# Differences of x by VectorE from two plain loads, EPS later, and the low parts of w_v ahead of the weight sums

## The chip, the cores and the metric

The kernel runs on one core of one Trainium2 chip. Its engines work side by side: TensorE (PE) multiplies matrices, VectorE (DVE) and ScalarE (ACT) work on elements, GpSimd (POOL) here issues the DMAs that add to what lies at their target, and SyncE (SP) issues the plain ones. Each engine takes its instructions strictly in order, so one that waits holds up all behind it. The metric is the device time of one execution in microseconds (us); lower is better.

## What is computed

One layer mixes a linear-attention block and a bilinear GLU by a gate per token. x has 2048 tokens of 512 numbers, all in fp32:

```
phi = lambda t: where(t > 0, t + 1, exp(t)) + 1e-6
q, k, v = x @ wqkv                      # 32 heads of 16
kv = einsum("bhsd,bhse->bhde", phi(k), v);   z = phi(k) summed over s
a = (phi(q) @ kv) / (phi(q) @ z + 1e-6) @ wo
b = ((x @ w_gate) * (x @ w_up)) @ w_down
g = sigmoid((x * gate_w).sum(-1))
out = g * a + (1 - g) * b
```

## The kernel before

Every fp32 operand is split into a high part that ACT writes and a low part that DVE gets by subtraction; `mm3` (L74) makes a product of three matmuls: high by high, high by low, low by high. Names that end in h or l are such parts (xc4h, wvl, fl). The large products are made by a 2x2 scheme with seven products instead of eight. Its operands of x are numbered 1 to 7 and taken in the order `UNIT = (2, 3, 4, 1, 5, 6, 7)`. Operands 2 and 5 are a block of x as it is; 1, 6 and 7 are sums of two blocks; 3 and 4 are differences (`SUMS`, L167).

The change touches **stage 1** alone (about the first 96 us): k and v of all 16 tiles of 128 tokens, phi of k, and the sums kv and z.
- First four "lead" tiles (8 to 11) go by plain products: pk with w_k, then pv with w_v.
- Then three pairs of couples go by the seven products. `couple` (L429) makes two tiles of tokens. Its step s multiplies one operand into a bank (cY, cX, cY, cR, cX, cR, cS), and `crit` moves it on: m copies the first cY on ACT, DVE makes cR from cX and m, t from cR and v, and cS from t and cX. Each step takes the product of both couples, one after the other.
- The first pair (tiles 12 to 15) uses "sub" operands, cut from the second half of the tokens: in SBUF as xo, and, split, in xb (xbh, xbl) or in soh and sol. The second and third pair (tiles 0 to 7) use the whole operands of the first half, which later serve stage 2 too: 2 and 7 in xa (xah, xal), 3 and 5 in xb, and 1, 4 and 6 in xc1, xc4 and xc6.

How an operand came about before: 3 and 4 (sub and whole) were loaded to xo, negated by ACT, and the other block was added by an accumulating DMA. The whole operands 2, 1, 5, 6 and 7 were first copied to a place in DRAM (xstage, `op_load`); where a sum was wanted, an accumulating DMA added the other block there (`op_add`), and `op_turn` (L417) fetched the result to SBUF when its place was free.

phi of a tile of k takes an exp (e) and a relu (ph) on ACT, two DVE instructions (ph, and zacc which sums for z), and last `phi_end` (L310), which adds EPS on ACT. A block of kv (pkv) needs the ended phi and v of its tiles.

The scheduling is by hand. `plan(step, fn)` puts a helper at a numbered half step of stage 1, from the table `AT`: `gsload`, `gsadd`, `gssplit` for sub operands, `goload`, `goadd`, `goturn`, `gosplit` for whole ones, `gwsplit` for sums of weights, `gkv` for kv. Steps 0 to 7 lie in the lead tiles, 8 to 21 in the first pair, 22 to 35 in the second, 36 to 49 in the third. Negative steps come ahead of all. `split_late` (L270) puts the high part at its place and the low part at the end of the half step's list. Buffers come from a list of 45 that is used in rotation (`get`, `put`), so a load also waits for the last reader of its buffer. `dma` (L82) goes through SP, `dma_add` (L85) through POOL. In the profile L52 is the matmul, L58 an ACT instruction, L61 and L64 DVE instructions.

Of the kernel before, what the change touches and what calls it, by code (L numbers as in the profile page):

```python
# [14 lines left out]
P = 128  # L15
# [8 lines left out]
CH = 512  # L24
# [12 lines left out]
UNIT = (2, 3, 4, 1, 5, 6, 7)  # L37
DOWN = (2, 6, 5, 7, 1, 3, 4)
STAYS = 1
AT = {'gsload': (-1, -1, -1, -1, -1, -1, -1), 'gsadd': (1, 0, 1, -1, 1, -1, 1), 'gssplit': (1, 3, 5, 7, 11, 13, 9), 'gmake': (-1, -1, -1, -1, -1, -1, -1, 5, -1, -1), 'gwsplit': (-1, -1, 7, 9, 11, 13, 12, 14, 15, 18), 'goload': (3, 9, 13, 7, 11, 11, 9), 'goadd': (3, 14, 17, 9, 1, 13, 17), 'gosplit': (13, 19, 25, 25, 30, 26, 30), 'gwgu': (31, 33, 49, 31, 39), 'gw0': (41, 42, 44, 42, 45, 47), 'gkv': (6, 14, 22, 27), 'by': ((16383, 10920, 10922, 10922, 2730, 10990), (8191, 10922, 10922, 10920, 11946, 10922)), 'add': (2, 4), 'high': ((2, 3, 5), (2, 3, 5), (2, 3, 4)), 'low': ((4, 4, 5), (3, 5, 6), (4, 4, 5)), 'd': (7, 8, 8, 9, 9, 9, 9, 15), 'h': (7, 7, 8, 8, 9, 13, 14, 13, 14, 15, 14, 15, 16, 15, 16, 17, 16, 17, 19), 'q0': (8, 8, 10, 11, 15, 21, 23, 24, 26, 58, 11, 11), 'q1': (8, 9, 10, 13, 24, 30, 32, 34, 38, 42, 3, 6), 'wo': (70, 6, 10, 7), 'x': (3, 4, 8, 8, 12, 12), 'o': (-3, -1, 0, 5, 35, 36, 37, 39), 'xs': (36, 41, 40, 0, 1, 2, 4), 'plain': (4, 7, 8, 1, 6, 7, 12, 12, 2, 6), 'turn': (14, 2, 18, 1, 38, 4, 50, 6), 'first': (0, 4, 1, 4, 6, 6, 14, 3, 5, 17, 15, 16, 19, 21), 'goturn': (7, 1, 5, 19, 19, 17, 20), 'gxload': (25, 27, 28, 29, 31, 34, 37, 39, 41, 43, 47, 49, 51, 54, 56, 58), 'gxsum': (32, 33, 35, 37, 33, 36, 39, 41, 43, 51, 55, 56, 57, 59, 67, 69)}  # L40


@with_exitstack
def gated_mix(ctx: ExitStack, tc, xt, xp, x, wqkv, wq, wq_add, wo, wgu, wgu_add, wdn, wdn_add, wdl, gate_w, out):
# [12 lines left out]
    def act(dst, src, func=AF.Copy, **kw):  # L57
        pin(nc.scalar.activation(dst, src, func, **kw))  # L58

    def tt(dst, a, b, op):  # L60
        pin(nc.vector.tensor_tensor(dst, a, b, op=op))  # L61
# [19 lines left out]
    def dma(dst, src):  # L81
        tc.keep_in_program_order(nc.sync.dma_start(dst, src))  # L82

    def dma_add(dst, src):
        tc.keep_in_program_order(nc.gpsimd.dma_start(dst, src, accum_op=ALU.add))  # L85
# [111 lines left out]
    def f32(w):  # L197
        return w.bitcast(F32)
# [12 lines left out]
    def later(slot, fn):  # L211
        at.setdefault(slot, []).append(fn)
# [53 lines left out]
    xs, phi, val = {}, {}, {}  # L266
# [67 lines left out]
    def plan(step, *fns):  # L334
        todo.setdefault(step, []).extend(fns)
# [33 lines left out]
        fac.setdefault(i, []).append(two)  # L369

    raw_op = {}
    xstage = {i: dram.tile([P, 2, CH], F32, name=f"xstage{i}") for i in (2, 1, 5, 6, 7)}

    def op_load(i):
        if i in xstage:
            dma(xstage[i], xp[0, SUMS[i][1]])
            return
        raw_op[i] = [get("xo") for _ in range(2)]
        for b in range(2):
            x_load(f32(raw_op[i][b]), 0, i, b)  # L380

    def op_add(i):
        if i in xstage:
            for b in range(2):
                dma_add(xstage[i][:, b], xp[0, SUMS[i][0]][:, b])
            return
        for b in range(2):
            x_add(f32(raw_op[i][b]), 0, i, b)

    ops_done = set()  # L390
    sub = {}
    PART = {A1: (B1, 0), A2: (B2, 0), B1: (B1, CH // 2), B2: (B2, CH // 2)}

    def pieces_of(w):
        return w.rearrange("p (b c) -> p b c", b=2)

    def sub_of(which):
        at_, col = PART[which]
        return xp[1, at_][:, :, col:col + CH // 2]

    def sub_load(i):
        sub[i] = get("xo")
        dma(pieces_of(f32(sub[i])), sub_of(SUMS[i][1]))

    def sub_add(i):
        one, _, minus = SUMS[i]
        if minus:
            act(f32(sub[i]), f32(sub[i]), scale=-1.0)
        dma_add(pieces_of(f32(sub[i])), sub_of(one))

    def sub_split(i):
        raw, n = sub[i], UNIT.index(i)
# [16 lines left out]
    def couple(c, tag):  # L429
        own_pair = c < KT  # L430
        ta, tb = (c, c + KT) if own_pair else (c + 8, c + 10)

        def bank_for(name):
            return unit_bank(name) if tag == "u" else bank_of("pd", name, 3)

        def operand(i, b):
            if own_pair:
                assert i in ops_done
                return [v[:, b, c * P:(c + 1) * P] for v in xc[i]]
            return [pieces_of(v)[:, b, (c - KT) * P:(c - KT + 1) * P] for v in sub[i]]  # L440

        bank, t = {}, {}

        def product(s):
            i, to = UNIT[s], "YXYRXRS"[s]
            first = i in (2, 3)
            assert len(fac[i]) == 2
            if first:
                bank[to] = bank_for(f"c{to}")
            for b in range(2):  # L450
                mm3(bank[to], operand(i, b), fac[i][b], first and b == 0, b == 1, not first, late=1)
            if not own_pair and c == KT + 1 and s > 3:
                put(*sub.pop(i))

        def crit(s):
            if s == 0:
                t["m2"] = get("m2")
                act(f32(t["m2"]), bank["Y"])
            elif s == 1:
                bank["R"] = bank_for("cR")  # L460
                tt(bank["R"], bank["X"], f32(t["m2"]), ALU.subtract)
                put(t["m2"])
            elif s == 2:
                val_of(ta, bank["Y"])
            elif s == 3:
                t["t"] = get("t")
                tt(f32(t["t"]), bank["R"], f32(val[ta]), ALU.add)
            elif s == 4:
                bank["S"] = bank_for("cS")
                tt(bank["S"], f32(t["t"]), bank["X"], ALU.subtract)  # L470
                put(t["t"])
                phi_k(tb, bank["X"])
            elif s == 5:
                phi_end(tb)
                val_of(tb, bank["R"])
            else:
                phi_k(ta, bank["S"])

        return product, crit, ta

    KV = (8, 9, 10, 11), (12, 14, 13, 15), (0, 4, 1, 5), (2, 6, 3, 7)

# [26 lines left out]
        plan(2 * n + 1, lambda t=t: phi_k(t, pk0[t]))  # L509
        plan(2 * n + 3, lambda t=t: phi_end(t))  # L510
    for k in range(KT):
        plan(-1, lambda k=k: split_v(k))
    for n, i in enumerate(UNIT):
        plan(G1["sload"][n], lambda i=i: sub_load(i))
        if i not in (2, 5):
            plan(G1["sadd"][n], lambda i=i: sub_add(i))
        plan(G1["ssplit"][n], lambda i=i: sub_split(i))
        plan(G1["oload"][n], lambda i=i: op_load(i))
        if i not in (2, 5):
            plan(G1["oadd"][n], lambda i=i: op_add(i))  # L520
        if i in xstage:
            plan(G1["oturn"][n], lambda i=i: op_turn(i))
        plan(G1["osplit"][n], lambda i=i: op_split(i))
# [48 lines left out]
    for two in (KT, KT + 1), (0, 1), (2, 3):  # L572
        pair_of = [couple(c, tag) for c, tag in zip(two, ("u", "pd"))]
        for s in range(7):
            now_slot[0] = step - STEPS
            extras(2 * step)
            for h, (product, crit, ta) in enumerate(pair_of):
                product(s)
                if h:
                    pair_of[0][1](s)  # L580
                elif s:
                    pair_of[1][1](s - 1)
                elif before:
                    last_plain()
                    before = None
                if s == 0 and ended:
                    phi_end(ended.pop(0))
                if not h:
                    kv_some(step)
            extras(2 * step + 1)  # L590
            step += 1
        ended = [ta for _, _, ta in pair_of]
        if two[0] != 2:
            pair_of[1][1](6)
    tail_crit = pair_of[1][1]
# [24 lines left out]

    begin = AT["first"]
    later(0, lambda: tail_crit(6))
    later(1, lambda: phi_end(2))
    later(1, lambda: phi_end(3))
    for s in range(step, step + 14):
        later(s - step, lambda s=s: kv_some(s))
    for k in range(2):
# [661 lines left out]
```

## Time and profile before

| | us |
|---|---|
| three runs | 593.53, 593.72, 595.69 |
| median | 593.72 |
| profiled execution | 593.48 |
| its span | 591.50 |
| second pair of couples, 50.09 to 75.17 | 25.08 |
| third pair of couples, 75.17 to 95.69 | 20.52 |

The span is what the trace covers; 1.98 us of the execution's time lie around it. All times on a trace count from the span's start. In a timeline a row reads: start, duration, engine, line, operation, what is written <- what is read, shape, and in brackets the idle time ahead of it and what ended it. In the list of waits a row reads: engine and instruction, what it waited for, us in total, times, longest. In the view by windows a row reads: stretch, its length, busy time of PE, weight loads, DVE, ACT and POOL with the count of instructions, then the clock that was granted to TensorE as a share of full speed, the DMA share and GB/s.

### The profile page before, as it was taken

The numbers are of one execution on the slowest core, as the hardware profiler recorded it, in microseconds if no ns is written. First come the engines' busy times: TensorE is split into PE (matmuls) and PEld (weight loads), VectorE is DVE, ScalarE is ACT, GpSimd is POOL, SyncE is SP. The second block draws the span as 40 slices with busy tenths as digits, with TensorE's granted clock in tenths as the row PEclk, the third lists the DMA queues.
The fourth block names the chain that finished last, engine by engine and source line by source line (L and its number), as shares of the span: only waits on it lengthen the run. The fifth ranks groups of instructions, "written<-read, shape, count | busy, mean of one in ns | idle before, by whom it ended". The sixth has DMA issues, their size and how long they took to land.

```text
span 591.5 us, 8699 instructions
## 1 busy us (share of the span) xinstructions
PE 582.2 (98%) x3047; PEld 474.6 (80%) x3047; DVE 505.0 (85%) x820; ACT 418.3 (71%) x755; POOL 67.3 (11%) x85
## 2 busy tenths in 40 slices
PE   8998999999999999999999999999999999999997
PEld 6785888777888888888888888888888888888885
DVE  7796687889698989998999976969899989889882
ACT  4588577879887878787974574887777677876300
POOL 0332000201111111111001100101101010100000
PEclk9999999999999999999999999999999999999999
DMA  8999674889797889878478356766847574631011
GB/s 280 227 271 235 205 169 148 196 209 222 183 251 178 213 203 242 192 183 212 109 219 218 115 133 188 150 139 149 188 106 162 150 159 116 134 81 35 1 74 69
DMA packets 45884, 99.29 MB, mean 168 GB/s; under 512 B 4384, under 2 KB 16928, under 8 KB 45728
## 3 DMA queue, kind: packets, MB, share of 16 engines
q0 software_dynamic: 11216, 37.49, 36.2%
q1 hardware_dynamic: 34336, 60.91, 30.0%
q8 instruction: 24, 0.39, 0.3%
q10 hardware_dynamic: 288, 0.33, 0.2%
q14 instruction: 20, 0.16, 0.1%
HBM read 87.43 MB, written 16.53 MB: 176 GB/s over the span
## 4 chain that ended last, share of the span: by engine, by line
PE 88%; ACT 4%; DMA 4%; DVE 2%; issue 1%; POOL 0%; SPq 0%; ACTq 0%; POOLq 0%
PE pdn L52 28%; PE bR L52 15%; PE bX L52 14%; PE bY L52 14%; PE bS L52 7%; PE pM L52 3%; DMA xo<-in_xp 2%; PE cR L52 2%; PE cY L52 2%; DMA wraw<-in_wqkv 2%; PE cX L52 1%; ACT e L58 1%; PE cS L52 1%; PE pkv L52 1%; ACT v L58 0%
## 5 line engine op out<-in xcount | busy, mean ns | idle before, releaser
L61 DVE TENSOR_TENSOR wcl<-wr,wch 128x512 fp32r<-128x512 f32 (+1 forms) x96 | 72.7, 772 | 5.2 <-ACT wch L58 5.2
L58 ACT ACTIVATE M<-pdn 128x512 f32<-128x512 f32 x84 | 49.9, 595 | 26.8 <-PE pdn L52 25.0
L52 PE MATMUL pdn<-hl,dh 128*128 128x512 f32 x176 | 68.5, 389 | 0.0
L52 PE MATMUL pdn<-hh,dh 128*128 128x512 f32 x176 | 68.5, 389 | 0.0
L52 PE MATMUL pdn<-hh,dl 128*128 128x512 f32 x176 | 68.5, 389 | 0.0
L58 ACT ACTIVATE wch<-wr 128x512 fp32r<-128x512 f32 (+1 forms) x96 | 66.7, 700 | 1.3 <-DMA wr<-in_wq_add 1.2
L61 DVE TENSOR_TENSOR M<-M,pdn 128x512 f32<-128x512 f32 x75 | 51.0, 681 | 13.9 <-PE pdn L52 13.7
L58 ACT ACTIVATE hh<-c 128x512 fp32r<-128x512 f32 x56 | 35.2, 629 | 37.0 <-DVE c L61 36.8
L85 POOL DMA_DIRECT2D wr<-in_wgu_add x28 | 24.3, 866 | 240.1 <-ACT wr L58 126.9
L52 PE MATMUL bX<-xbh,wch 128*128 128x512 f32 x128 | 49.8, 389 | 0.0
L52 PE MATMUL bX<-xbh,wcl 128*128 128x512 f32 x128 | 49.8, 389 | 0.0
L52 PE MATMUL bX<-xbl,wch 128*128 128x512 f32 x128 | 49.8, 389 | 0.0
L58 ACT ACTIVATE pdn<-M 128x512 f32<-128x512 f32 x61 | 35.9, 589 | 11.7 <-DVE M L61 11.7
L52 PEld LDWEIGHTS pdn<-hh,dh 128*128 128x128 f32 x176 | 33.0, 188 | 7.0
L52 PEld LDWEIGHTS pdn<-hl,dh 128*128 128x128 f32 x176 | 33.0, 188 | 7.0
L61 DVE TENSOR_TENSOR hl<-c,hh 128x512 fp32r<-128x512 f32 x56 | 38.3, 684 | 0.4
L52 PEld LDWEIGHTS pdn<-hh,dl 128*128 128x128 f32 x176 | 33.0, 188 | 6.8
L58 ACT ACTIVATE wr<-wr 128x512 f32<-128x512 f32 x64 | 36.7, 627 | 0.0
L61 DVE TENSOR_TENSOR dl<-dr,dh 128x512 fp32r<-128x512 f32 (+1 forms) x40 | 29.7, 764 | 2.3 <-ACT dh L58 2.1
L58 ACT ACTIVATE c<-bX 128x512 f32<-128x512 f32 x28 | 16.8, 600 | 20.0 <-DVE bS L61 20.0
L58 ACT ACTIVATE m<-bY 128x512 f32<-128x512 f32 x32 | 18.9, 591 | 16.5 <-PE bY L52 16.5
L58 ACT ACTIVATE dh<-dr 128x512 fp32r<-128x512 f32 (+1 forms) x40 | 27.1, 685 | 4.1 <-PE pdn L52 3.4
(265 smaller groups left out, 1597.3 us busy)
## 6 DMA issues: line engine op xcount, KB each, us to landing
wr<-in_wgu_add POOLq DMA_DIRECT2D x28, 640.0 KB, 6.4
wr<-in_wgu SPq DMA_DIRECT2D x28, 384.0 KB
dr<-in_wdn_add POOLq DMA_DIRECT2D x12, 640.0 KB, 6.9
dr<-in_wdn SPq DMA_DIRECT2D x12, 384.0 KB
xraw<-in_x SPq DMA_DIRECT2D x16, 256.0 KB
terms<-zq SPq DMA_DIRECT2D x16, 256.0 KB
zt<-terms SPq DMA_DIRECT2D x16, 256.0 KB
rb<-den SPq DMA_DIRECT2D x16, 256.0 KB
```

What stands on the lines that cost most here:

```text
L52: tc.keep_in_program_order(nc.tensor.matmul(*args, **kw))
L58: pin(nc.scalar.activation(dst, src, func, **kw))
L61: pin(nc.vector.tensor_tensor(dst, a, b, op=op))
L85: tc.keep_in_program_order(nc.gpsimd.dma_start(dst, src, accum_op=ALU.add))
```

## The change

- Of the operands of stage 1, 3 and 4 are made by DVE. Both of their blocks are loaded plainly to SBUF, and `tt(..., ALU.subtract)` takes the difference in place. The second block of each is operand 5 or 2 itself (`WITH = {4: 2, 3: 5}`), so these two are no longer loaded separately: their copies to DRAM and their turns are gone. This holds for the sub operands and for the whole ones.
- `phi_end` of the tiles of a pair of couples moves from inside the pair to steps 1 and 2 of the next pair, and after the last pair to the first two slots of stage 2. The kv blocks move a step later (`gkv`).
- The splits of w_v are planned at step -3, ahead of the sums of weights at -1.
- Loads, additions, splits and turns of the operands get new steps.

```diff
 AT = {
...
-  'gwsplit': (-1, -1, 7, 9, 11, 13, 12, 14, 15, 18),
-  'goload': (3, 9, 13, 7, 11, 11, 9), 'goadd': (3, 14, 17, 9, 1, 13, 17),
-  'gosplit': (13, 19, 25, 25, 30, 26, 30), 'gkv': (6, 14, 22, 27), 'goturn': (7, 1, 5, 19, 19, 17, 20)
+  'gwsplit': (-1, -1, 7, 9, 11, 13, 12, 14, 15, 16),
+  'goload': (0, 11, 5, 7, 0, 9, 9), 'goadd': (0, 14, 8, 9, 0, 12, 14),
+  'gosplit': (11, 19, 10, 23, 25, 27, 28), 'gkv': (6, 15, 22, 28), 'goturn': (0, 0, 0, 17, 0, 17, 20)
...
-    xstage = {i: dram.tile([P, 2, CH], F32, name=f"xstage{i}") for i in (2, 1, 5, 6, 7)}
+    xstage = {i: dram.tile([P, 2, CH], F32, name=f"xstage{i}") for i in (1, 6, 7)}
+    WITH = {4: 2, 3: 5}

     def op_load(i):
...
-        raw_op[i] = [get("xo") for _ in range(2)]
+        for k in (i, WITH[i]):
+            raw_op[k] = [get("xo") for _ in range(2)]
+            for b in range(2):
+                dma(f32(raw_op[k][b]), xp[0, SUMS[i][k != i]][:, b])
+
+    def op_add(i):
         for b in range(2):
-            x_load(f32(raw_op[i][b]), 0, i, b)
...
+            if i in xstage:
                 dma_add(xstage[i][:, b], xp[0, SUMS[i][0]][:, b])
-            return
-        for b in range(2):
-            x_add(f32(raw_op[i][b]), 0, i, b)
+            else:
+                tt(f32(raw_op[i][b]), f32(raw_op[i][b]), f32(raw_op[WITH[i]][b]), ALU.subtract)
...
     def sub_load(i):
-        sub[i] = get("xo")
-        dma(pieces_of(f32(sub[i])), sub_of(SUMS[i][1]))
+        for k in (i, WITH[i]) if i in WITH else (i,):
+            sub[k] = get("xo")
+            dma(pieces_of(f32(sub[k])), sub_of(SUMS[i][0 if k == i and i in WITH else 1]))

     def sub_add(i):
-        one, _, minus = SUMS[i]
-        if minus:
-            act(f32(sub[i]), f32(sub[i]), scale=-1.0)
-        dma_add(pieces_of(f32(sub[i])), sub_of(one))
+        if i in WITH:
+            tt(f32(sub[i]), f32(sub[i]), f32(sub[WITH[i]]), ALU.subtract)
+        else:
+            dma_add(pieces_of(f32(sub[i])), sub_of(SUMS[i][0]))
...
             elif s == 5:
-                phi_end(tb)
                 val_of(tb, bank["R"])
...
-        plan(-1, lambda k=k: split_v(k))
+        plan(-3, lambda k=k: split_v(k))
...
-                if s == 0 and ended:
+                if s in (1, 2) and ended:
                     phi_end(ended.pop(0))
...
-        ended = [ta for _, _, ta in pair_of]
+        ended = [ts[k] for k in range(2) for _, _, ts in pair_of]
...
-    later(1, lambda: phi_end(2))
-    later(1, lambda: phi_end(3))
+    for k, t in enumerate(ended):
+        later(k // 2, lambda t=t: phi_end(t))
```

What this makes of the order on the engines is seen at three places. The first is on DVE, at the beginning (from about 11 us): wkl and wvl are low parts of w_k and w_v, ws and early are sums of weights, f2l the low part of the first of these; xo<-xo is a subtraction of sub operands.

```order
 L61 TENSOR_TENSOR wkl<-wraw,wkh 128x512
+L61 TENSOR_TENSOR wvl<-wraw,wvh 128x512 x4
 L61 TENSOR_TENSOR ws<-wraw 128x512 x4
 L61 TENSOR_TENSOR early<-wraw 128x512 x3
 L61 TENSOR_TENSOR ws<-wraw 128x512 x2
-L61 TENSOR_TENSOR wvl<-wraw,wvh 128x512 x4
 L61 TENSOR_TENSOR f2l<-ws,f2h 128x512 x2
```

The four wvl pass the nine sums; behind f2l, where ph and zacc of the first lead tile stood, xo<-xo, ph and zacc, and again xo<-xo stand now.

The second place is on DVE too, in the first pair of couples. fl are low parts of sums of weights, sol of sub operands; the two cR are those of the two couples.

```order
 L61 TENSOR_TENSOR fl<-ws,fh 128x512
+L61 TENSOR_TENSOR xo<-xo 128x512 x2
 L61 TENSOR_TENSOR sol<-xo,soh 128x512
 L61 TENSOR_TENSOR fl<-ws,fh 128x512
-L61 TENSOR_TENSOR cR<-cX,m_391 128x512
+L61 TENSOR_TENSOR xc4l<-xo,xc4h 128x512 x2
+L61 TENSOR_TENSOR cR<-cX,m_395 128x512
+L61 TENSOR_TENSOR xal<-xo,xah 128x512 x2
 L61 TENSOR_TENSOR sol<-xo,soh 128x512
 L61 TENSOR_TENSOR fl<-ws,fh 128x512
 L61 TENSOR_TENSOR fl<-early,fh 128x512
-L61 TENSOR_TENSOR cR<-cX,m_416 128x512
```

Ahead of the second cR there are six instructions more: two differences for operand 4, its two low parts, and the two low parts of operand 2, which stood behind it.

The third place is on ACT, at the same time. The rows are those from the first m to where the second cR's m stands.

```order
 L58 ACTIVATE soh<-xo 128x512
 L58 ACTIVATE fh<-ws 128x512
-L58 ACTIVATE m_416<-cY 128x512
+L58 ACTIVATE xc4h<-xo 128x512 x2
+L58 ACTIVATE m_421<-cY 128x512
+L58 ACTIVATE xah<-xo 128x512 x2
 L58 ACTIVATE soh<-xo 128x512
 L58 ACTIVATE fh<-ws 128x512
```

The high parts of operand 4 stand here now; before they stood in the second pair, behind both of its m.

More of the change, by code (lines that the diff above doesn't have):

```diff
@@ L39 @@
 STAYS = 1
-AT = {'gsload': (-1, -1, -1, -1, -1, -1, -1), 'gsadd': (1, 0, 1, -1, 1, -1, 1), 'gssplit': (1, 3, 5, 7, 11, 13, 9), 'gmake': (-1, -1, -1, -1, -1, -1, -1, 5, -1, -1), 'gwsplit': (-1, -1, 7, 9, 11, 13, 12, 14, 15, 18), 'goload': (3, 9, 13, 7, 11, 11, 9), 'goadd': (3, 14, 17, 9, 1, 13, 17), 'gosplit': (13, 19, 25, 25, 30, 26, 30), 'gwgu': (31, 33, 49, 31, 39), 'gw0': (41, 42, 44, 42, 45, 47), 'gkv': (6, 14, 22, 27), 'by': ((16383, 10920, 10922, 10922, 2730, 10990), (8191, 10922, 10922, 10920, 11946, 10922)), 'add': (2, 4), 'high': ((2, 3, 5), (2, 3, 5), (2, 3, 4)), 'low': ((4, 4, 5), (3, 5, 6), (4, 4, 5)), 'd': (7, 8, 8, 9, 9, 9, 9, 15), 'h': (7, 7, 8, 8, 9, 13, 14, 13, 14, 15, 14, 15, 16, 15, 16, 17, 16, 17, 19), 'q0': (8, 8, 10, 11, 15, 21, 23, 24, 26, 58, 11, 11), 'q1': (8, 9, 10, 13, 24, 30, 32, 34, 38, 42, 3, 6), 'wo': (70, 6, 10, 7), 'x': (3, 4, 8, 8, 12, 12), 'o': (-3, -1, 0, 5, 35, 36, 37, 39), 'xs': (36, 41, 40, 0, 1, 2, 4), 'plain': (4, 7, 8, 1, 6, 7, 12, 12, 2, 6), 'turn': (14, 2, 18, 1, 38, 4, 50, 6), 'first': (0, 4, 1, 4, 6, 6, 14, 3, 5, 17, 15, 16, 19, 21), 'goturn': (7, 1, 5, 19, 19, 17, 20), 'gxload': (25, 27, 28, 29, 31, 34, 37, 39, 41, 43, 47, 49, 51, 54, 56, 58), 'gxsum': (32, 33, 35, 37, 33, 36, 39, 41, 43, 51, 55, 56, 57, 59, 67, 69)}
@@ new lines @@
+AT = {'gsload': (-1, -1, -1, -1, -1, -1, -1), 'gsadd': (1, 0, 1, -1, 1, -1, 1), 'gssplit': (1, 3, 5, 7, 11, 13, 9), 'gmake': (-1, -1, -1, -1, -1, -1, -1, 5, -1, -1), 'gwsplit': (-1, -1, 7, 9, 11, 13, 12, 14, 15, 16), 'goload': (0, 11, 5, 7, 0, 9, 9), 'goadd': (0, 14, 8, 9, 0, 12, 14), 'gosplit': (11, 19, 10, 23, 25, 27, 28), 'gwgu': (31, 33, 49, 31, 39), 'gw0': (41, 42, 44, 42, 45, 47), 'gkv': (6, 15, 22, 28), 'by': ((16383, 10920, 10922, 10922, 2730, 10990), (8191, 10922, 10922, 10920, 11946, 10922)), 'add': (2, 4), 'high': ((2, 3, 5), (2, 3, 5), (2, 3, 4)), 'low': ((4, 4, 5), (3, 5, 6), (4, 4, 5)), 'd': (7, 8, 8, 9, 9, 9, 9, 15), 'h': (7, 7, 8, 8, 9, 13, 14, 13, 14, 15, 14, 15, 16, 15, 16, 17, 16, 17, 19), 'q0': (8, 8, 10, 11, 15, 21, 23, 24, 26, 58, 11, 11), 'q1': (8, 9, 10, 13, 24, 30, 32, 34, 38, 42, 3, 6), 'wo': (70, 6, 10, 7), 'x': (3, 4, 8, 8, 12, 12), 'o': (-3, -1, 0, 5, 35, 36, 37, 39), 'xs': (36, 41, 40, 0, 1, 2, 4), 'plain': (4, 7, 8, 1, 6, 7, 12, 12, 2, 6), 'turn': (14, 2, 18, 1, 38, 4, 50, 6), 'first': (0, 4, 1, 4, 6, 6, 14, 3, 5, 17, 15, 16, 19, 21), 'goturn': (0, 0, 0, 17, 0, 17, 20), 'gxload': (25, 27, 28, 29, 31, 34, 37, 39, 41, 43, 47, 49, 51, 54, 56, 58), 'gxsum': (32, 33, 35, 37, 33, 36, 39, 41, 43, 51, 55, 56, 57, 59, 67, 69)}
@@ L377, in op_load @@
             return
-        raw_op[i] = [get("xo") for _ in range(2)]
+        for k in (i, WITH[i]):
[3 more added lines that the diff above has]
+    def op_add(i):
         for b in range(2):
-            x_load(f32(raw_op[i][b]), 0, i, b)
-    def op_add(i):
-        if i in xstage:
-            for b in range(2):
+            if i in xstage:
                 dma_add(xstage[i][:, b], xp[0, SUMS[i][0]][:, b])
-            return
-        for b in range(2):
-            x_add(f32(raw_op[i][b]), 0, i, b)
+            else:
+                tt(f32(raw_op[i][b]), f32(raw_op[i][b]), f32(raw_op[WITH[i]][b]), ALU.subtract)
     ops_done = set()
@@ L477, in crit @@
                 phi_k(ta, bank["S"])
-        return product, crit, ta
+        return product, crit, (tb, ta)
     KV = (8, 9, 10, 11), (12, 14, 13, 15), (0, 4, 1, 5), (2, 6, 3, 7)
@@ L511, in gated_mix @@
     for k in range(KT):
-        plan(-1, lambda k=k: split_v(k))
-    for n, i in enumerate(UNIT):
-        plan(G1["sload"][n], lambda i=i: sub_load(i))
+        plan(-3, lambda k=k: split_v(k))
+    for n, i in sorted(enumerate(UNIT), key=lambda p: p[1] not in WITH):
         if i not in (2, 5):
+            plan(G1["sload"][n], lambda i=i: sub_load(i))
             plan(G1["sadd"][n], lambda i=i: sub_add(i))
         plan(G1["ssplit"][n], lambda i=i: sub_split(i))
-        plan(G1["oload"][n], lambda i=i: op_load(i))
         if i not in (2, 5):
+            plan(G1["oload"][n], lambda i=i: op_load(i))
             plan(G1["oadd"][n], lambda i=i: op_add(i))
@@ L576, in gated_mix @@
             extras(2 * step)
-            for h, (product, crit, ta) in enumerate(pair_of):
+            for h, (product, crit, _) in enumerate(pair_of):
                 product(s)
```

## Prediction

> **What bounds the kernel now.** First the shares, and the chain that ended last:
>
> ```profile
> PE 582.2 (98%) x3047; PEld 474.6 (80%) x3047; DVE 505.0 (85%) x820; ACT 418.3 (71%) x755; POOL 67.3 (11%) x85
> ...
> PE 88%; ACT 4%; DMA 4%; DVE 2%; issue 1%; POOL 0%; SPq 0%; ACTq 0%; POOLq 0%
> ```
>
> TensorE (PE) is the bound nearly everywhere. A busier or idler VectorE (DVE) or ScalarE (ACT) counts only where PE waits. So the second view is the list of PE's waits, and the third is its timeline where they fall, all in stage 1:
>
> ```profile
> PE cY L52 <- ACT xc4h L58: 2.1, 1, 2.1
> ...
> PE pv L52 <- DVE wvl L61: 0.5, 1, 0.5
> ```
> ```profile
> 17.09 0.39 PE L52 MATMUL pv<-wvh,xal 128*128 128x512 f32 x1
> 17.98 0.50 PE L52 MATMUL pv<-wvl,xah 128*128 128x512 f32 x1 [0.51 <-DVE wvl L61]
> 18.32 0.39 PE L52 MATMUL pv<-wvh,xah 128*128 128x512 f32 x1
> ...
> 39.50 0.39 PE L52 MATMUL cR<-fh,xbh 128*128 128x512 f32 x1
> ...
> 46.30 0.39 PE L52 MATMUL cS<-fh,soh 128*128 128x512 f32 x1
> ...
> 48.60 0.50 PE L52 MATMUL cS<-fh,soh 128*128 128x512 f32 x1
> ...
> 50.09 0.39 PE L52 MATMUL cY<-f2h,xah 128*128 128x512 f32 x1
> ...
> 55.31 0.39 PE L52 MATMUL cX<-wkl,xbh 128*128 128x512 f32 x1
> 57.80 0.49 PE L52 MATMUL cY<-wvh,xc4h 128*128 128x512 f32 x1 [2.10 <-ACT xc4h L58]
> 58.52 0.79 PE L52 MATMUL cY<-wvh,xc4l 128*128 128x512 f32 x1 [0.23 <-DVE xc4l L61]
> ...
> 62.63 0.39 PE L52 MATMUL cR<-fh,xc1h 128*128 128x512 f32 x1
> ```
> ```profile
> 75.17 2.72 PE cY L52 x12
> ...
> 95.69 1.36 PE bY L52 x6
> ```
>
> Columns are start, duration and work. Twelve matmuls take 2.72 us, so one is due every 0.227 us, and whatever is longer between two starts is loss:
> - **pv:** 17.09 to 18.32 is 1.23 us for two steps, 0.78 lost.
> - **cS:** 46.30 to 50.09 is 3.79 us for twelve matmuls, 1.07 lost. The second couple's six start only at 48.60.
> - **xc4:** the matmul after 55.31 was due at 55.54 and came at 57.80 (2.26 lost); the next came after 0.72 (0.49 lost); then 58.52 to 62.63 is 4.11 us for eleven steps that should take 2.50 (1.61 lost). Together 4.36. That last part is the clock:
>
> ```profile
> 47.00:48.00 1.00, 0.87 (x4) 0.30 (x3) 0.86 (x3) 0.22 (x1) 1.00 (x3) 1.00 1.09 197
> ...
> 59.00:60.00 1.00, 1.00 (x4) 0.71 (x4) 1.00 (x3) 1.00 (x3) 0.00 (x0) 0.50 0.21 43
> ```
>
> The third value from the end is the granted clock: half at 59 us, after the 2.1 us wait, but full at 47 us, where the gaps are short. The second pair of couples runs from 50.09 to 75.17 (25.08 us), the third, with the same number of products and one kv block, from 75.17 to 95.69 (20.52). The difference, **4.56 us**, is all that the second pair loses; 4.36 of it is explained above.
>
> **The change, part by part.** Why was xc4h late? These are ACT, then DVE, then SyncE (SP) and GpSimd (POOL):
>
> ```profile
> 26.29 0.63 ACT L58 ACTIVATE xbh<-xo 128x512 fp32r<-128x512 f32 x1 [3.02 <-DMA xo<-in_xp]
> ...
> 28.88 0.64 ACT L58 ACTIVATE xbh<-xo 128x512 fp32r<-128x512 f32 x1
> ...
> 39.69 1.21 ACT L58 ACTIVATE xo<-xo 128x512 f32<-128x512 f32 x2
> ...
> 48.64 0.60 ACT L58 ACTIVATE e<-cX 128x512 f32<-128x512 f32 x1 [1.42 <-DVE cS L61]
> ...
> 49.61 0.73 ACT L58 ACTIVATE e<-ph,epsc 128x512 f32<-128x512 f32 x1
> 50.23 0.60 ACT L58 ACTIVATE v<-cR 128x512 f32<-128x512 f32 x1
> ...
> 57.13 1.14 ACT L58 ACTIVATE xc4h<-xo 128x512 fp32r<-128x512 f32 x2
> ```
> ```profile
> 11.82 2.49 DVE L61 TENSOR_TENSOR ws<-wraw 128x512 f32<-128x512 f32 x4
> ...
> 17.24 2.49 DVE L61 TENSOR_TENSOR wvl<-wraw,wvh 128x512 fp32r<-128x512 f32 x4
> 19.66 1.28 DVE L61 TENSOR_TENSOR f2l<-ws,f2h 128x512 fp32r<-128x512 f32 x2
> 20.86 0.68 DVE L64 SCALAR_TENSOR_TENSOR ph<-e,ph 128x512 f32<-128x512 f32 x1
> ...
> 22.18 0.68 DVE L61 TENSOR_TENSOR xbl<-xo,xbh 128x512 fp32r<-128x512 f32 x1
> ...
> 31.62 0.69 DVE L64 SCALAR_TENSOR_TENSOR ph<-e,ph 128x512 f32<-128x512 f32 x1
> ...
> 38.38 0.69 DVE L61 TENSOR_TENSOR cR<-cX,m 128x512 f32<-128x512 f32 x1
> ...
> 43.86 0.68 DVE L61 TENSOR_TENSOR cS<-t,cX 128x512 f32<-128x512 f32 x1
> 45.69 0.69 DVE L64 SCALAR_TENSOR_TENSOR ph<-e,ph 128x512 f32<-128x512 f32 x1 [1.15 <-ACT ph L58]
> ...
> 47.86 0.69 DVE L61 TENSOR_TENSOR cS<-t,cX 128x512 f32<-128x512 f32 x1
> ```
> ```profile
> 27.54 0.53 SPq L82 DMA_DIRECT2D xstage<-in_xp  x1
> ...
> 34.56 1.70 POOL L85 DMA_DIRECT2D xstage<-in_xp  x2 [11.10 <-DMA xstage<-in_xp]
> ```
>
> From 48.64 to 57.13 ACT runs without a gap, and xc4h stands behind four phi_end's and two m's. In the changed order both xc4h stand ahead of m_421, where they need only four plain loads and two DVE subtractions.
>
> *Low parts of w_v first.* The four wvl move ahead of nine sums; the total is unchanged, and f2l still starts at 19.66. One DVE instruction takes 0.60 us from start to start (two f2l, 19.66 to 20.86). wvl now starts at 11.82 and all four are done by 14.3, against a need at 17.3: the 0.78 us is removed there. The sums end 2.4 us later, and raw buffers come free then, at about 19.7; the loads of operands 4 and 2 wait for those.
>
> *Sub-operands 3 and 4.* Out go two ACT negations and two accumulating DMAs (the sub-operands' five become three). In come two DVE subtractions, 1.20 us. DVE has no idle room from 11.8 to 20.9, so the phi of the first lead tile starts at 21.5, not 20.86. But ACT no longer waits until 26.29 for an accumulation. Its cycle per lead tile is 28.88 - 26.29 = 2.59 us; started by that phi at 22.2, it puts the three xbh at 23.8, 26.3 and 28.9, against 26.29, 28.88 and 31.44 (one cycle on). DVE's cycle fits: a ph and zacc pair is 22.18 - 20.86 = 1.32, and two more make 2.5. So DVE's last lead ph stands at 29.0, not 31.62: 2.6 us gained.
>
> *Then DVE pays it back.* Between that ph and the second cR the new order has the pair and fourteen others: 29.03 + 1.32 + 14 x 0.60 = **38.8**, with 0.69 more until it is written (39.5); before it started at 38.38. The additions are two xo, two xc4l and two xal, all ahead of the second cR. PE, 0.78 earlier, would want that bank at 38.72 (39.50 - 0.78). It waits **0.8 us**, and the pv gain is gone. From the second cR to the first cS two xo and an fl come in and the two xal are gone: ten steps, 44.8 against 43.86. ACT's e and ph follow that cS (43.86 to 45.69, 1.83), then DVE's pair 1.32: the second cS starts at 44.8 + 1.83 + 1.32 = 47.95, against 47.86. It is usable at 48.7; PE has finished the first couple's six at 47.66. **PE waits 1.03 us** there, nearly the same loss as the 1.07 before, by another cause. The second pair so starts at about 50.1, as it does now.
>
> *Operands 4 and 2, 3 and 5.* Both copies to DRAM, their turns and the accumulations go, with four ACT negations (two in 1.21 at 39.69); four subtractions on DVE come. A staged copy issued at 27.54 had landed at 34.56, 7.0 us; I take that for a plain load of half the size, which bounds it from above; anything quicker changes nothing, as xc4h is not waited for. Issued by 20.4, the loads are there by 27.4. DVE asks for them at 31.6, four us later. xc4h then runs at 32.6, twenty us before its need at 55.5. **The whole stall goes, with its half clock.** POOL issues nothing for 3 and 4, SP is no longer held by the turn of operand 2 (which waited for PE to finish with xa), and the copies of 1, 6 and 7 start some 6 us earlier, at 21.
>
> *EPS later.* Nothing is saved in total; a phi_end is 50.23 - 49.61 = 0.62 us, and four of them move behind the m's. What is late next? ACT from 48.7: without four phi_end and one m the 8.49 us to 57.13 becomes 5.5, so xc1h starts at 54.2, xc1l on DVE ends at 56.7 and the two cR at 57.3 and 59.4. PE wants them at 50.1 + 3 x 2.72 = 58.3 and, for the second couple, 59.6. That is 0.2 to 1 us of room: cost 0 to 0.3 us, I take 0. kv blocks move one step, behind other matmuls: nothing.
>
> **Sum.** -0.78 + 0.80 (pv, cR), -1.07 + 1.03 (cS), -4.56 (second pair), 0 after it, where PE has no wait over 0.2 us: **-4.6 us**. The profiled execution is 593.48 us (span 591.50), 0.24 below the median of 593.72. 593.48 - 4.56 gives 588.9; with the median's offset 589.2. I say **589.0**.
>
> **Rivals.**
> - *More is kept.* DVE turns out not to hold PE; the first two losses vanish too: 589.0 - 1.8 = 587.2. Against it: DVE's order is a chain of counted steps. Chance 0.10.
> - *The clock falls again.* A gap of 0.5 us left it full, one of 2.1 halved it; the new single gaps, 0.8 and 1.03, lie between. The price is that of the row at 59 us, 1.6: 590.6, with both 592.2. Nearer to the gaps that did no harm in all, so 0.17. The Trainium skill (TensorE: Matmul & The Clock Gate, Part 1: The HAM clock gate) says that the clock halves after at least one idle window of about 3.4 us. By that rule this rival has no chance, but nor would the 2.1 us wait have halved it, and it did: the trace speaks against the rule's threshold, so the rival stays.
> - *The wait moves to the next operand.* xc1h or the second cR comes 1 to 2 us late, the clock falls, and the second pair loses 2 to 4 us again: 591 to 593. For it: the room is 0.2 us at cR. Chance 0.08.
> - *Slower.* The eight plain loads stand on SP around the copies of 1, 6 and 7; those land late, their accumulations and turns later, and ACT, in order, stops at xc1h with everything behind it. It costs from the moment the turn lands after 56, one us for one, and makes the kernel over 0.5% slower from 63.5 on (7.5 us late), with 597 or more. Against it: before, copies issued from 27.5 had their turns issued at about 48; now they start 6 us earlier and carry less with them, so the turns land near 48. Chance 0.05.
> - *It does not do what it says:* the last two cover it; xc4 itself is early by twenty us.
>
> **How the numbers follow.** The forecast's own range is 588 to 590, chance 0.60. A measurement of this kernel can tell about 0.5%, 3.0 us, from no change, so faster means below 590.7. Faster: 0.60 + 0.10 + half of the clock's 0.17 = 0.78. Same: the other half and the next-operand case, 0.17. Slower: 0.05. The range 587.0 to 592.0 holds the first two and most of the clock's; some 0.17 is left out.
>
> **What would show it.** Right: no PE wait on xc4h; clock 1.00 throughout 50 to 70; PE waits on DVE cR near 39 (0.8) and cS near 48 (1.0); pv without a wait; the first bY near 91. Wrong: a half clock in any of those; a PE wait on xc1 or on a cR after 50; DVE idle between 29 and 38; an ACT wait on a DMA at xc1h.

## The result and the profile after

The changed kernel takes 590.87 us (median of 5 runs, 589.39 to 591.78), against 594.69 (593.53 to 595.69) for the kernel before, run beside it: a ratio of **0.9937, 95% interval 0.9915 to 0.9958**. The forecast was 589.0, in a range of 587.0 to 592.0. The profiled execution took 590.87 us with a span of 589.1; before it was 593.48 and 591.50. So the two traces differ by 2.4 us of span, less than the medians do.

First the shares of the engines and of the chain that ended last, of the kernel after:

```profile
PE 578.9 (98%) x3047; PEld 473.4 (80%) x3047; DVE 508.3 (86%) x826; ACT 415.1 (70%) x749; POOL 61.5 (10%) x79
...
PE 90%; DMA 5%; DVE 2%; ACT 1%; SPq 1%; issue 1%; POOL 0%; DVEq 0%; ACTq 0%
```

PE is busy for 3.3 us less (582.2 before) with as many matmuls; the half clock that is gone is part of that. ACT's share of the chain fell, that of DMA rose. Next PE's waits in stage 1, from the list of waits:

```profile
PE cY L52 <- ACT m L58: 1.7, 1, 1.7
...
PE cR L52 <- DVE cR L61: 1.7, 1, 1.7
...
PE cS L52 <- DVE cS L61: 0.7, 1, 0.7
```

The waits for xc4h and at pv are gone. In their place stand three in the first pair of couples; the forecast had two, 0.8 at cR and 1.03 at cS. The chain that ended last shows what stands ahead of the second pair:

```profile
17.65 1.59 POOL xo L85 x2
19.24 15.03 DMA xo<-in_xp
```

PE's timeline shows the starts of the second and the third pair; the first row is the start of the third pair in the kernel before, the other two are of the kernel after. Then a row of the view by windows, after:

```profile
75.01 0.39 PE L52 MATMUL cY<-f2h,xah 128*128 128x512 f32 x1
```
```profile
52.41 0.39 PE L52 MATMUL cY<-f2h,xah 128*128 128x512 f32 x1
...
72.98 0.39 PE L52 MATMUL cY<-f2h,xah 128*128 128x512 f32 x1
```
```profile
50.00:60.00 10.00, 9.33 (x42) 7.54 (x41) 8.16 (x14) 9.05 (x18) 0.00 (x0) 1.00 0.20 61
```

The second pair now takes 20.57 us (52.41 to 72.98). Before, it took 24.92 (50.09 to 75.01): the 25.08 given for it takes its start from the timeline and its end, 75.17, from the chain, where a row begins only when the matmul ahead has ended, 0.16 us after the next one has started. So **4.35 us are gone there**, and the clock in the row of the windows is 1.00. But the pair starts at 52.41, not at 50.09: 2.32 us are lost ahead of it. ACT's and DVE's timelines show where:

```profile
28.89 0.68 ACT L58 ACTIVATE xbh<-xo 128x512 fp32r<-128x512 f32 x1
...
34.30 0.63 ACT L58 ACTIVATE soh<-xo 128x512 fp32r<-128x512 f32 x1 [2.62 <-DMA xo<-in_xp]
...
35.35 1.13 ACT L58 ACTIVATE xc4h<-xo 128x512 fp32r<-128x512 f32 x2
```
```profile
29.09 0.69 DVE L64 SCALAR_TENSOR_TENSOR ph<-e,ph 128x512 f32<-128x512 f32 x1
...
31.63 1.28 DVE L61 TENSOR_TENSOR xo<-xo 128x512 f32<-128x512 f32 x2
34.96 0.69 DVE L61 TENSOR_TENSOR sol<-xo,soh 128x512 fp32r<-128x512 f32 x1 [2.05 <-ACT soh L58]
...
40.98 0.69 DVE L61 TENSOR_TENSOR cR<-cX,m 128x512 f32<-128x512 f32 x1
...
47.00 0.68 DVE L61 TENSOR_TENSOR cS<-t,cX 128x512 f32<-128x512 f32 x1
...
50.17 0.69 DVE L61 TENSOR_TENSOR cS<-t,cX 128x512 f32<-128x512 f32 x1
```

Up to 31.6 both engines keep the forecast's timetable to 0.1 us (28.9 for the third xbh, 29.0 for the last lead ph, 31.6 for the two xo). Then ACT stands for 2.62 us at the first soh. That is the high part of sub operand 7, a sum, which an accumulating DMA makes, and the DMA has not landed. DVE waits 2.05 us behind it, and all that follows is late by this: the second cR by 2.2 (38.8 was forecast), the two cS by 2.2 too. Here is what was on the way then, as POOL and SP issued it, and the DMA engines' load:

```profile
17.65 3.50 POOL L85 DMA_DIRECT2D xo<-in_xp  x3 [15.82 <-DMA xo<-in_xp]
```
```profile
20.73 1.97 SPq L82 DMA_DIRECT2D xstage<-in_xp  x3
22.80 4.54 SPq L82 DMA_DIRECT2D xo<-in_xp  x4
```
```profile
25.00:30.00 5.00, 5.00 (x24) 4.14 (x23) 4.44 (x8) 5.00 (x11) 0.00 (x0) 1.00 1.22 402
```

Sub operand 7 is the third of POOL's three additions (1, 6, 7). Right behind its issue come the copies of 1, 6 and 7 to DRAM and four plain loads. The share of the DMA engines from 25 to 30 us is 1.22, at 402 GB/s.

**Theory:** the lost 2 us are this accumulation; without its wait the forecast's steps and its 589.0 hold. **First rival:** DVE's longer chain loses them anyway, wherever ACT stands. **Second rival:** EPS or w_v costs or brings what the forecast took for nothing.

### The profile page after: what moved, and what is told of

The parts are those of the page before. It is cut to its first block, busy times and chain, and to the rows that moved or that the text cites. A ratio compares the mean times of both kernels' runs of the same rounds, so it can differ in the third digit from the quotient of the medians.

```text
span 589.1 us, 8688 instructions
## 1 busy us (share of the span) xinstructions
PE 578.9 (98%) x3047; PEld 473.4 (80%) x3047; DVE 508.3 (86%) x826; ACT 415.1 (70%) x749; POOL 61.5 (10%) x79
## 4 chain that ended last, share of the span: by engine, by line
PE 90%; DMA 5%; DVE 2%; ACT 1%; SPq 1%; issue 1%; POOL 0%; DVEq 0%; ACTq 0%
PE pdn L52 28%; PE bR L52 15%; PE bY L52 15%; PE bX L52 15%; PE bS L52 7%; DMA xo<-in_xp 4%; PE pM L52 3%; PE cX L52 2%; PE cR L52 2%; PE cY L52 2%; PE cS L52 1%; DMA wraw<-in_wqkv 1%; PE pkv L52 1%; DVE fl L61 1%; ACT e L58 0%
```

## Experiments

The kernel before was run in each of the three sets: median 593.55 for the first four kernels, 594.13 for the next four, 592.68 for the last two; beside the changed kernel itself it was 594.69. Between sets the ratios are therefore compared, which refer to the runs of the same set. They carry the scatter of the kernel before (590.93 to 596.55 in the first set), so a difference of a few tenths of a us between two sets says little.

### Sub operand 7 ahead of 6

```diff
-  'gsadd': (1, 0, 1, -1, 1, -1, 1),
+  'gsadd': (1, 0, 1, -1, 1, 1, -1),
```

> The changed kernel, with the accumulating DMA of sub operand 7 issued ahead of that of 6 (their order on POOL is 1, 7, 6 instead of 1, 6, 7). Theory A: the 2.6 us that ACT waits at soh (until 34.3) for sub operand 7 is what keeps the change from its full gain, because DVE, in order, stops 2.05 us at sol and both cR come late. Then soh is waited for by 1 us or less, the second cR starts at 39 to 40.5 instead of 40.98, and the time falls by 0.5 to 2 us against the changed kernel's 590.9. If the third add is slow because of what else is in flight and not because it stands third, 6 now lands at 34 and is late for its own split, which is due about 2 us later, so most is gained all the same. Theory B: DVE's count of instructions ahead of the second cR is the bound, the wait at soh lies beside it: the time stays within 0.4 us of 590.9.

Measured: 588.99 us (588.83 to 589.58), ratio 0.9925 (0.9912 to 0.9938). ACT's soh, DVE's cR and cS, PE's waits and the starts of the pairs:

```profile
31.48 0.69 ACT L58 ACTIVATE soh<-xo 128x512 fp32r<-128x512 f32 x1
```
```profile
38.83 0.69 DVE L61 TENSOR_TENSOR cR<-cX,m 128x512 f32<-128x512 f32 x1
...
44.84 0.68 DVE L61 TENSOR_TENSOR cS<-t,cX 128x512 f32<-128x512 f32 x1
...
48.01 0.69 DVE L61 TENSOR_TENSOR cS<-t,cX 128x512 f32<-128x512 f32 x1
```
```profile
PE cR L52 <- DVE cR L61: 1.8, 1, 1.8
...
PE cS L52 <- DVE cS L61: 0.7, 1, 0.7
```
```profile
50.25 0.39 PE L52 MATMUL cY<-f2h,xah 128*128 128x512 f32 x1
...
70.82 0.39 PE L52 MATMUL cY<-f2h,xah 128*128 128x512 f32 x1
```

Nothing but the order of two additions has changed. soh has no wait, and DVE stands where the forecast put it: 38.8, 44.8 and 47.95 were its numbers. The second pair starts 2.16 us earlier than in the changed kernel and takes the same 20.57. The first rival falls: DVE's chain costs what was counted and no more.

How much of this every execution loses is less sure than how. The traces differ by 2.1 us of span, the medians by 1.9, but the ratios by only 0.0012, 0.7 us, and their intervals overlap. All five runs of this kernel lie within 0.75 us, those of the changed one within 2.4, so a wait that is longer in some executions than in others would fit; only profiled executions show it.

### The copies to DRAM later

The additions keep their order; the copies of 1, 6 and 7, with their additions, are issued later.

```diff
-  'goload': (0, 11, 5, 7, 0, 9, 9), 'goadd': (0, 14, 8, 9, 0, 12, 14),
+  'goload': (0, 9, 5, 11, 0, 11, 11), 'goadd': (0, 14, 8, 12, 0, 12, 14),
```

> The changed kernel, with the three copies of operands 1, 6 and 7 to DRAM (3 x 512 KB) behind the four loads for operands 3 and 5 on SP, which pushes them from 20.7 us to about 30. Theory A with contention: the accumulating DMA of sub operand 7, issued at 19 to 21, lands at 34.3 because plain transfers take the DMA engines; without the copies it lands by 30, ACT does not wait at soh, and the time falls by 1 to 2.5 us against 590.9. If POOL's own issue were slow instead, it still lands near 34 and nothing is gained. What is at risk: the turns of 1, 6 and 7 come 8 us later, at 47 to 55, and ACT may wait at xc1h (due at 54 to 56); then the second pair loses what the first gains.

Measured: 589.02 us (588.60 to 590.03), ratio 0.9927 (0.9911 to 0.9943). SP, a window, ACT, and the time from issue to landing of the three additions to xo:

```profile
32.18 1.84 SPq L82 DMA_DIRECT2D xstage<-in_xp  x3
45.33 0.34 SPq L82 DMA_DIRECT2D xc1l<-xstage  x1
```
```profile
25.00:30.00 5.00, 5.00 (x24) 4.14 (x23) 4.44 (x8) 5.00 (x11) 0.00 (x0) 1.00 0.51 144
```
```profile
31.56 0.69 ACT L58 ACTIVATE soh<-xo 128x512 fp32r<-128x512 f32 x1
```
```profile
DMA to landing us min/median/max: 4.2/8.3/10.2
```

Operand 7 is third again and is there in time, with the DMA share from 25 to 30 us at 0.51 instead of 1.22. In this execution POOL's additions began at 16.39, not 17.65, but that does not decide it: from issue to landing no addition took more than 10.2 us, against 15.0 for that of operand 7 in the changed kernel. Issued at 18.0 it was there by 28.2, and 1.3 us later it would still be in time for 31.5. So the copies made the accumulation late; one kernel that goes against this stands in the last section. The turn of operand 1, issued at 45.33 instead of 38.85, is not waited for.

### The low parts of w_v alone, on the kernel before

```diff
-        plan(-1, lambda k=k: split_v(k))
+        plan(-3, lambda k=k: split_v(k))
```

> The kernel before with one part of the change alone: the low parts of w_v ahead of the sums of weights. The prediction's step says that the wait of 0.5 us (0.78 lost) at pv goes, and that nothing of it is left at the end of the first pair of couples, since the chain of DVE and ACT up to the second cS sets that end: the time stays within 0.4 us of the kernel before. Rival: the 0.78 us stays won, the time falls by 0.8 us.

Measured: 593.35 us (12 runs, 591.03 to 595.57), ratio 1.0 (0.9983 to 1.0017). PE's waits, and the clock behind the longer one:

```profile
PE cY L52 <- ACT xc4h L58: 2.1, 1, 2.1
...
PE cY L52 <- ACT m L58: 1.1, 1, 1.1
```
```profile
60.00:61.00 1.00, 1.00 (x4) 0.76 (x3) 1.00 (x3) 0.66 (x2) 0.00 (x0) 0.50 0.67 184
```

The wait at pv is gone; a new one for m and the old ones for cS and xc4h take it all: in the chain the third pair starts at 75.15, against 75.17 before. The edit alone brings nothing.

### EPS as before, in the changed kernel

```diff
             elif s == 5:
+                phi_end(tb)
...
-                if s in (1, 2) and ended:
+                if s == 0 and ended:
...
-        ended = [ts[k] for k in range(2) for _, _, ts in pair_of]
+        ended = [ts[1] for _, _, ts in pair_of]
...
-        later(k // 2, lambda t=t: phi_end(t))
+        later(1, lambda t=t: phi_end(t))
```

> The changed kernel with EPS put back to where it was before (phi_end inside the pair and at step 0 of the next). The theory that EPS later is what makes room for operand 1 in the second pair: four phi_end of 0.62 us stand ahead of xc1h again, xc1h starts at 58.5 instead of 56.3, PE waits 1 to 2 us at the cR of the second pair or for its operand xc1, and the time rises by 1 to 2 us to about 592.4. Rival: ACT has room enough there, PE does not wait, the time stays within 0.4 us of 590.9.

Measured: 591.58 us (12 runs, 590.76 to 594.38), ratio 0.9975 (0.9961 to 0.9990), 0.0038 above the changed kernel. PE's waits:

```profile
PE cY L52 <- ACT m L58: 1.0, 2, 0.6
...
PE bR L52 <- DVE bR L61: 0.5, 1, 0.5
```

xc1h and the two cR of the second pair cause no wait, which was the place the forecast had looked at. PE waits instead for the two m of the second pair, behind the ended phi's, and for bR, where stage 2 begins. The medians differ by 0.7 us only (590.87 and 591.58), but this execution waited less for operand 7, and its second pair started at 51.10 instead of 52.41. By PE's timeline that pair takes 22.17 us (51.10 to 73.27) instead of 20.57, and from there to the kv block of stage 2 it is 0.3 us more: 1.9 us in all.

### The same, with sub operand 7 ahead

The diff is that of the experiment before, on the kernel with 7 ahead of 6.

> The kernel of e1_seven_first (588.99 us) with EPS put back to where it was before. On this base nothing waits at soh, so the price of that part is seen by itself. Theory: in e4_eps_undone PE waited 0.52 and 0.77 at the second cY of the second pair, for the m that stands behind four phi_end on ACT, and 0.64 at bR at the beginning of stage 2; together 1.9 us. Then the time here is 590.4 to 591.2, with these waits. Rival: these waits came from the late ACT of that run, the time stays within 0.4 us of 588.99.

Measured: 591.23 us (12 runs, 590.70 to 593.38), ratio 0.9965 (0.9948 to 0.9981), 0.0040 (2.4 us) above the kernel with 7 ahead. The profiled execution is its slowest. PE's waits:

```profile
PE cY L52 <- ACT m L58: 0.9, 2, 0.6
...
PE bR L52 <- DVE bR L61: 0.7, 2, 0.5
```

The same two places; the second pair takes 22.10 us (51.17 to 73.27) instead of 20.57, and with the 0.3 us at stage 2 that is 1.8 us. Moving EPS is worth about 2 us on the changed kernel, whichever order the additions have. Beside it the order of the additions brings 0.0010 here, 0.6 us, so the average gain from it is again smaller than in the traces.

### The low parts of w_v late again, with sub operand 7 ahead

```diff
-        plan(-3, lambda k=k: split_v(k))
+        plan(-1, lambda k=k: split_v(k))
```

> The kernel of e1_seven_first (588.99 us) with the splits of w_v back at the sums of weights. Theory: the wait at pv comes back (0.78 us lost), and PE, later by that much, waits 1.0 instead of 1.8 us for the second cR; DVE's chain to the second cS (48.0) is the same, so the time stays within 0.4 us of 588.99. Rival: each part of the change adds its gain, the time rises by 0.8 us.

Measured: 589.74 us (588.72 to 590.15), ratio 0.9929 (0.9905 to 0.9952), against 0.9925. PE's waits, and DVE's second cS:

```profile
PE pv L52 <- DVE wvl L61: 1.0, 1, 1.0
```
```profile
48.03 0.69 DVE L61 TENSOR_TENSOR cS<-t,cX 128x512 f32<-128x512 f32 x1
```

PE waits 1.0 us at pv and in return not at cR; the second cS stands at 48.03 against 48.01, and the second pair starts at 50.26 against 50.25. The median is 0.75 us higher, the ratio by 0.0004, 0.2 us. So this part of the change is worth nothing up to the second pair, and nothing that the intervals can tell: DVE's chain sets the end of the first pair, and PE can wait in one place or the other.

### Four low parts moved out of that chain

If DVE's chain sets the end, shortening it must pay. The low parts of operands 4 and 2 (four instructions ahead of the second cR) are kept back and put between the first cS and its phi, and the second cS and its phi, where DVE waited 1.15 us for ACT. This and the next two kernels have 7 ahead of 6.

```diff
-    def split_late(hi, lo, raw, free=()):
+    kept = {}
+
+    def split_late(hi, lo, raw, free=(), to=None):
...
-        lows.append(low)
+        (lows if to is None else to).append(low)
...
-    def phi_k(t, bank):
+    def phi_k(t, bank, fill=()):
...
+        for fn in fill:
+            fn()
...
-            split_late(*[v[:, b] for v in xc[i]], f32(w), [w])
+            split_late(*[v[:, b] for v in xc[i]], f32(w), [w], kept.setdefault(i, []) if i in (2, 4) else None)
...
-                phi_k(tb, bank["X"])
+                phi_k(tb, bank["X"], kept.pop({KT: 2, KT + 1: 4}.get(c), ()))
```

> The kernel of e1_seven_first (588.99 us) with the four low parts of operands 2 and 4 taken out of DVE's chain: they stand in the two gaps in which DVE waits for ACT's e and ph, behind the first and the second cS of the first pair. Theory: DVE's count of instructions sets the second cR and both cS; four times 0.60 us less puts the second cR at 36.4 instead of 38.83 and the second cS at 45.6 instead of 48.0; PE does not wait at cR and less than 0.7 us at cS, and the time falls by 1.8 to 2.6 us to 586.4 to 587.2. Rival: the cS are bound by ACT or by PE's own products, the time falls by less than 0.6 us. A third: operands 1 or 3 come late for the earlier second pair (xc1h, xbl), and half of it is lost again.

Measured: 588.50 us (588.06 to 589.13), ratio 0.9913 (0.9892 to 0.9934). DVE:

```profile
35.66 0.69 DVE L61 TENSOR_TENSOR sol<-xo,soh 128x512 fp32r<-128x512 f32 x1 [1.10 <-ACT soh L58]
...
37.47 0.69 DVE L61 TENSOR_TENSOR cR<-cX,m 128x512 f32<-128x512 f32 x1
```

A miss: the second cR came at 37.47, not 36.4, and the median fell by 0.5 us, not by 1.8 to 2.6. With four steps (2.4 us) gone from DVE, ACT became the limit: DVE waits 1.10 us for the second soh, which stands behind the high parts of 4 and 2 on ACT.

### Sub operand 7 made by DVE

Its two blocks are already in SBUF, one as the first block of operand 4, the other as operand 5, so neither a load nor an accumulation is needed, but DVE gets one instruction more.

```diff
-  'gsadd': (1, 0, 1, -1, 1, -1, 1),
+  'gsadd': (1, 0, 1, -1, 1, -1, 0),
...
+        if i == 7:
+            sub[i] = get("xo")
+            return
...
-        if i in WITH:
+        if i == 7:
+            tt(f32(sub[7]), f32(sub[4]), f32(sub[5]), ALU.add)
+        elif i in WITH:
```

> The changed kernel with sub operand 7 made by DVE as the sum of two blocks that lie in SBUF already (A2 and B2), without its load and its accumulating DMA: one more DVE instruction of 0.60 us at about 21 us. Theory: ACT cannot wait for that DMA any longer, and every instruction in DVE's chain costs its 0.60 us at the end of the first pair: the second cR starts at 39.4, the second cS at 48.6, and the time is 589.6, that is 0.6 above e1_seven_first (588.99) and 1.3 below the changed kernel. Rival: the chain is not counted so strictly, the time equals that of e1_seven_first within 0.3 us.

Measured: 590.05 us (588.97 to 592.19), ratio 0.9940 (0.9917 to 0.9964). DVE of this kernel, then the same first row of the kernel with 7 ahead:

```profile
11.37 2.49 DVE L61 TENSOR_TENSOR wvl<-wraw,wvh 128x512 fp32r<-128x512 f32 x4
...
38.99 0.69 DVE L61 TENSOR_TENSOR cR<-cX,m 128x512 f32<-128x512 f32 x1
```
```profile
11.81 2.49 DVE L61 TENSOR_TENSOR wvl<-wraw,wvh 128x512 fp32r<-128x512 f32 x4
```

From wvl to the second cR is 27.62 us against 27.02: one DVE instruction more, 0.60 us, arrives there in full. There is no accumulation to wait for, yet this is not better than issuing it in the right order.

### The high parts out of the way too

The kernel with the four low parts moved, and the high parts of 2 and 4 moved as well, to steps 15 and 16, near the two cS, for which ACT waits.

```diff
-  'gosplit': (11, 19, 10, 23, 25, 27, 28),
+  'gosplit': (15, 19, 16, 23, 25, 27, 28),
```

> The kernel of e7_lows_in_gaps (588.5 us) with the high parts of operands 2 and 4 moved on ACT too, from between the soh of the first pair to the 4 us in which ACT waits for the first cS. In e7 the four low parts gave 1.1 us instead of 2.4, because DVE then waited 1.10 us at sol for the second soh, which stands behind xc4h, m and xah on ACT. Theory: with the high parts gone from there ACT is no longer the limit: no wait at that sol, the second cR 36.4, the second cS 45.6, PE waits less than 0.7 us at cS, and the time falls by 0.9 to 1.4 us to 587.1 to 587.6. Rival: the accumulating DMA of sub operand 6 (third on POOL) or the loads of operands 3 and 5 are waited for at once, now that DVE and ACT come earlier, and less than 0.4 us is gained.

Measured: **587.34 us (586.99 to 587.90), ratio 0.9896 (0.9874 to 0.9918)**. DVE:

```profile
36.38 0.69 DVE L61 TENSOR_TENSOR cR<-cX,m 128x512 f32<-128x512 f32 x1
...
43.11 0.69 DVE L61 TENSOR_TENSOR cS<-t,cX 128x512 f32<-128x512 f32 x1
...
46.34 0.69 DVE L61 TENSOR_TENSOR cS<-t,cX 128x512 f32<-128x512 f32 x1
```

The second cR comes 2.45 us earlier than with 7 ahead alone. The two cS come 0.7 us behind what was expected, since DVE waits for a high part of weights from ACT; the second stands 1.67 us earlier than with 7 ahead alone. This is the lowest median of all the kernels tried.

### That kernel with the copies late

The diff is that of the second experiment.

> The kernel of e9_highs_late_too with the copies of operands 1, 6 and 7 behind the loads of 3 and 5, as in e2_copies_late. If e9 is held up by DMAs (sub operand 6, or operands 3 and 5), this is faster by what it waited there; if not, it is the same within 0.4 us, or slower by up to 1 us where the turns, which come later, are waited for at xc1h.

Measured: 587.70 us (586.90 to 588.69), ratio 0.9902 (0.9881 to 0.9924): the same. Once 7 goes ahead of 6, the copies do no harm to the time. They still slow the additions: with the copies early (POOL began at 17.21) the slowest of the three took 13.4 us from issue to landing, here (17.12) it took 10.3.

## Why the prediction was right, and where it was off

- **The stall at xc4h: right.** It was to bring 4.56 us, half clock included; the second pair shows 4.35, which is the 4.36 that the forecast had listed loss by loss (the 0.2 us more in its 4.56 come for the most part of mixing the two views). But the forecast gave all of it to the earlier xc4h and took EPS as neutral ("Nothing is saved in total"). Putting EPS back costs some 2 us, 1.6 of it in that same pair: on ACT three phi_end of 0.62 us then stand ahead of its first m and a fourth ahead of the second. The rest of the change, without EPS later, brings 2.75 us there (24.92 to 22.17).
- **Not tested: EPS later alone, on the kernel before.** Its four phi_end stand ahead of xc4h too. Without them xc4h could run at 57.13 - 4 x 0.62 = 54.7, or when its two additions are there: issued at 46.47 and 47.01, with 7.0 and 9.1 us to landing, so between 53.5 and 56.1. This is an estimate from these rows. PE wanted xc4h at 55.5, so moving EPS may have removed most of that stall without any subtraction on DVE. What the subtractions are worth by themselves stays open.
- **pv gained and given back at cR: right.** With w_v's low parts late again the time is the same within the intervals. The wait at cR was 1.8 us, not 0.8, in the kernel with 7 ahead. The forecast took PE's arrival from the trace of before; in this execution PE had come to pv earlier (15.75 against 16.86). DVE's finish, not PE's arrival, sets the end, so this did no harm to the sum.
- **DVE's chain of counted steps: right**, to 0.1 us over the sixteen instructions to the second cR and on to both cS, once nothing interrupts it (38.83, 44.84 and 48.01 against 38.8, 44.8 and 47.95).
- **The step that was mis-sized** is "Between that ph and the second cR the new order has the pair and fourteen others", with the waits 0.80 and 1.03 at cR and cS that follow from it. It counted instructions and took sub operand 7 as there. Among the transfers it weighed the plain loads and, in the rival "Slower", the copies as far as xc1h. It did not ask whether the accumulation that ACT needs at 31.5 would share the DMA engines with copies that the change starts 6 us earlier. It landed at 34.3, and the second pair, which was to start "at about 50.1, as it does now", started at 52.41 in the profiled execution. With 7 ahead of 6 it starts at 50.25, and the median is 588.99 against 589.0; that the two agree to 0.01 us is chance, since the sum's 4.56 was 0.2 too large.
- **The range: held in part by luck.** The 590.87 lies 1.9 us above the 589.0 and outside the forecast's own 588 to 590. The room up to 592.0 had been left for a fall of the clock, which the profiled execution does not show; what used it was a DMA that the forecast had not weighed.
- **The rivals.** "More is kept" falls: DVE does hold PE. "The clock falls again" falls in the profiled execution: there the clock stayed at 1.00 through stage 1. "The wait moves to the next operand" was wrong in its place: xc1h ran at 56.3 without a wait, and at 54.14 with 7 ahead, where 54.2 was forecast. The mechanism of "Slower", a DMA made late by the copies, came true, but at another operand and for 2 us instead of 8.

Open is how long the wait at soh is on average: it costs 0.7 us by the ratios and 1.9 by the medians, 2.1 in the profiled pair. That it varies is seen in the profiled execution with EPS as before, whose ACT waits less for the same transfer:

```profile
32.99 0.63 ACT L58 ACTIVATE soh<-xo 128x512 fp32r<-128x512 f32 x1 [1.50 <-DMA xo<-in_xp]
```

## What to carry to other kernels

When a change moves copies or loads earlier, list every transfer that is in flight then and the instruction that waits for each, the accumulating ones first; not only the transfers that were moved. When an engine's chain has been counted step by step and agrees, the next gain is in taking steps out of it, and then out of the engine that feeds it: the low parts alone brought 1.4 us at the second cR, low and high parts together 2.45. An edit that removes a wait of an engine that waits again shortly after is worth nothing by itself.

## What the hardware did that was not expected

**Waits of 2.08 and 2.10 us halved the clock, waits of up to 1.95 us did not.** PE's wait of 2.08 us in the kernel before with w_v's low parts first ended at 57.63 and left a granted clock of 0.50 at 60 us; the 2.10 us of the kernel before, which ended at 57.80, left 0.50 at 59 us. The changed kernel's two waits of 1.7 us and the 1.95 us at cR in the kernel with 7 ahead and EPS as before, which ended at 40.48, did not:

```profile
PE cR L52 <- DVE cR L61: 1.9, 1, 1.9
```
```profile
41.00:42.00 1.00, 1.00 (x6) 0.78 (x6) 1.00 (x3) 1.00 (x3) 0.00 (x0) 1.00 1.11 197
42.00:43.00 1.00, 1.00 (x6) 0.84 (x5) 1.00 (x3) 0.15 (x1) 0.00 (x0) 1.00 1.07 266
```

The Trainium skill (TensorE: Matmul & The Clock Gate, Part 1: The HAM clock gate) has a window of about 3.4 us of idleness; the two waits that halved the clock are shorter than that. Whether the length decides, between 1.95 and 2.08 us, or also where the wait falls, no run here tells. The kernel before does not lose its clock every time: of the 23 executions of the first set six have a mean granted clock of 0.999 or 1.000 and take 590.93 to 592.86 us, the other 17 have 0.995 to 0.998 and take 592.39 to 596.55. How long PE waited in each is not recorded. So part of the gain over the median of the kernel before is a half clock that most of its executions have, but not all.

**An accumulating transfer of 256 KB took twice its usual time.** In the kernel before nine such additions to xo had these times from issue to landing:

```profile
DMA to landing us min/median/max: 4.3/7.5/9.1
```

In the changed kernel the third took 15.0 us (19.24 to 34.3), with 402 GB/s of copies, loads and additions on the way from 25 to 30 us; with the copies later and 144 GB/s the slowest took 10.2. The other kernels go the same way: with the copies early the slowest of the three took 13.2 to 14.4 us in five more kernels, with the copies late 10.3 in one. One goes against it: with w_v's low parts late again the copies were issued at 20.99, and all three additions landed within 9.7 us. What tips it is not shown.
